# Softmax attention with a highway layer on one core: batch 1's attention moved behind the first chunk's products, its query scaled by head halves on two engines, and the last output tiles on more banks

## The chip, the cores and the metric

The kernel runs on one core of one Trainium2 chip. The metric is device time in microseconds. A core has TensorE (PE, which multiplies and transposes into PSUM), VectorE (DVE), ScalarE (ACT), GpSimd (POOL) and SyncE (SP, which here issues nearly all transfers); each works through its own list of instructions in order, and waits on semaphores where a result of another engine is needed.

## The reference

q, k and v have 8 batches, 8 heads, 576 positions and 64 features. The result of the attention goes, position by position, through a highway layer of width 512 (8 heads by 64).

```python
q_s = softmax(q, axis=-1)            # over the 64 features
k_s = softmax(k, axis=2)             # over the 576 positions
kv  = einsum('bhsd,bhse->bhde', k_s, v)
x   = einsum('bhsd,bhde->bhse', q_s, kv)   # then to [8*576, 512]
H   = maximum(x @ w_h, 0)
T   = sigmoid(x @ w_t + b_t)
out = T * H + (1 - T) * x
```

## The kernel before

A batch's q, k and v come as one tile each: 64 position groups of two heads on the 128 partitions, and 4 head pairs by 9 positions by 64 features in a row. Matmuls take 16-bit inputs.

Attention of batch `b`, by helper:

- `exp_half(b, which, a)`: ACT takes the exponential of one half of q or k (`eq`, `ek`), two head pairs at a time.
- `q_sums(b, a)`: DVE sums the 64 features of one half (tile `r32`). `q_scale_v` (batches 0 to 2) takes the reciprocal, copies it to 16 bits (`r2`) and scales all of `eq` on DVE in two pieces, 1024 and 1280 elements; from batch 3 on, POOL scales (`q_recip`, `q_scale_p`).
- `cast_v`: POOL converts v in halves to `v16`.
- `q_trans(b, g)`: PE transposes `eq` in three groups of positions (4, 4 and 1; tiles `pq`), and DVE copies each into `qsT`.
- `kv_half`, `kv_norm`: PE multiplies k and v (`psk`), DVE normalises it into `kvn`.
- `x_pair`, `x_left`: PE multiplies `qsT` and `kvn` (`px`). For the first 8 position groups the result goes to `xT`, three casts by ACT and one by DVE; the ninth group of every batch is collected in `x9`.

The highway layer works on nine chunks: chunk `c` below 8 is batch `c`'s `xT`, chunk 8 is `x9`. For each of four output blocks `ob`, `gate` has PE multiply by the gate's weights (`pt`) and ACT take a tanh in place, `carry` has PE multiply by the other weights (`ph`) and DVE form `dd = max(ph, 0) - x`, and `blend` has DVE form `g = (th + 1) * dd`. `out_tile(g, n)` turns x and half of `g` of two batches back into rows on PE (tile `nat`, eight matmuls in a pair of weights each), ACT copies it to `o32`, and after four tiles SP sends 1 MB off. `turn9` and `finish9` do that for chunk 8, with one `o9` tile for each pair of batches and transfers issued by SP and ACT.

PSUM has eight banks: four of `ps_ht` (tag `ht`) for `pt` and `ph`, three of `ps_q` (tag `qx`) for `pq`, `psk` and `px`, and one of `ps_nat` (tag `nat`). Tiles of a tag take its banks in turn, and a bank is free again once its last reader is done.

The order is written out by hand. `at(p, ...)` puts work at a place in a list, with place `8*c + 2*ob` for the gate of chunk `c` and block `ob`, the next for its carry, and two later its blend; the attention of batch `b` lies between the products of chunk `b - 1`. The list is then run once, which sets the order on every engine. Tiles of loaded data have three buffers for each of q, k and v; SP's loads run ahead as far as those allow.

Of the kernel before, what the change touches and what calls it, by code (L numbers as in the profile page):

```python
# [9 lines left out]
FP32 = mybir.dt.float32  # L10
FP16 = mybir.dt.float16
# [7 lines left out]
def kernel(  # L19
# [19 lines left out]
    def heads_view(t, b):  # L39
# [3 lines left out]
    consts = pool("consts", 1)  # L43
# [3 lines left out]
    small = pool("small", 2)  # L47
# [4 lines left out]
    og = pool("og", 2)  # L52
    ps_ht = pool("ps_ht", 4, space=PSUM)
    ps_q = pool("ps_q", 3, space=PSUM)
    ps_nat = pool("ps_nat", 1, space=PSUM)
# [4 lines left out]
        o, l, r, start=st, stop=sp, skip_group_check=True  # L60
    )

    def ptrans(o, i):
        nc.tensor.matmul(  # L64
            o, i, ident, is_transpose=True, start=True, stop=True,
            skip_group_check=True,
        )
# [9 lines left out]
    x9 = consts.tile([P, 4, B, 64], FP16, name="x9")  # L77
    g9 = consts.tile([P, 4, B, 64], FP16, name="g9")
# [68 lines left out]
    ek, eq, psk, qsT = {}, {}, {}, {}  # L147
# [45 lines left out]
    qsum = {}  # L193
# [9 lines left out]
    def q_scale_v(b):  # L203
# [7 lines left out]
        for s in (slice(0, 16), slice(16, 4 * N9)):  # L211
            nc.vector.tensor_mul(e[:, s], e[:, s], rb[:, s])  # L212

    def q_recip(b):
        nc.vector.reciprocal(qsum[b], qsum[b])  # L215

# [3 lines left out]
        r = qsum[b][:, s]  # L220
        nc.gpsimd.tensor_mul(e, e, r.broadcast_to(list(e.shape)))  # L221
# [90 lines left out]
    o32 = {}  # L312
    rows = out.rearrange("(g p n) m -> g p n m", g=B // 2, n=N9)

    def turn_block(t, k_, xs, us):
        dst = t[:, k_, :]
        mm(dst, xs, ident, True, False)
        mm(dst, us, half_i, False, True)

    def flat(t):  # L320
        return t.rearrange("p k d -> p (k d)")

    def out_tile(g, n):
# [9 lines left out]
        nc.scalar.copy(o32[g, n // 4][:, n % 4, :], flat(t))  # L333
# [4 lines left out]
    nat9 = {}  # L338

    def turn9(k_):  # L340
        for g in range(B // 2):
            if k_ == 0:
                ps, tag = (ps_q, "qx") if g < 3 else (ps_ht, "ht")
                nat9[g] = ps.tile([P, 4, P], FP32, tag=tag, name=f"nat9_{g}")
            blk = lambda t: t[:, k_, 2 * g : 2 * g + 2].rearrange("p b d -> p (b d)")
            turn_block(nat9[g], k_, blk(x9), blk(g9))

    o9 = {}

    def finish9(ks):  # L350
        c = slice(128 * ks[0], 128 * ks[-1] + 128)
        for g in range(B // 2):
            if g not in o9:
                o9[g] = og.tile([P, 512], FP32, tag="o9", bufs=4, name=f"o9_{g}")
            if g % 2:
                nc.vector.tensor_copy(o9[g][:, c], flat(nat9[g])[:, c])
            else:
                nc.scalar.copy(o9[g][:, c], flat(nat9[g])[:, c])
            (nc.sync, nc.scalar)[g % 2].dma_start(rows[g][:, NM, c], o9[g][:, c])


    events = {}
# [23 lines left out]
    for k_ in range(4):  # L386
        at(8 * B + 2 * k_ + 2, E(turn9, k_))
    at(8 * B + 7, E(finish9, (0, 1, 2)))
    at(8 * B + 8, E(finish9, (3,)))

    for b in range(1, B):
        p = 8 * (b - 1)
        s = p + {1: -1, 2: -2, 3: -4}.get(b, -5)
        if b > 1:
            at(s, E(exp_half, b, "q", 0))
        at(s + 1, E(exp_half, b, "q", 1), E(q_sums, b, 0))
        at(s + 2, E(q_sums, b, 1))
        if b <= 2:
# [25 lines left out]
    for f in [  # L424
        E(warm_up, 20),
        E(exp_half, 0, "q", 0), E(q_sums, 0, 0),
        E(exp_half, 0, "q", 1), E(q_sums, 0, 1),
        E(q_scale_v, 0),
        E(exp_half, 0, "k", 0), E(cast_v, 0, 0),
        E(exp_half, 0, "k", 1), E(cast_v, 0, 1),  # L430
        E(q_trans, 0, 0), E(q_trans, 0, 1), E(warm_up, 2), E(q_trans, 0, 2),
        E(warm_up, 6),
        E(kv_half, 0, 0), E(gate_bias), E(warm_up, 2), E(kv_half, 0, 1), E(kv_norm, 0),
        E(warm_up, 4),
        E(x_pair, 0, 0), E(warm_up, 2), E(x_pair, 0, 1), E(warm_up, 2), E(x_left, 0),
        E(warm_up, 2),
        *[E(cast_weight, "t", k_, nc.vector) for k_ in range(4)],
        *[E(cast_weight, "h", k_, (nc.gpsimd, nc.vector)[k_ // 3]) for k_ in range(4)],
        E(exp_half, 1, "q", 0),
    ]:  # L440
        f()
# [34 lines left out]
```

## Time and profile before

| | |
|---|---|
| median of 7 runs | 150.5 us (150.26 to 150.72) |
| the profiled execution | 150.53 us, of which the span is 148.6 us |
| busy in the span | PE 122.9 us (83%), DVE 107.0 (72%), ACT 89.5 (60%), POOL 40.6 (27%) |
| granted clock of PE, mean | 0.964 |
| transfers | 40.06 MB, of which 30.41 MB read and 9.44 MB written |

The span runs from the first to the last instruction. A busy share is an average over the whole of it, and the stages differ: the first third loads and starts up, the middle runs one chunk after another, and the last 20 us finish the last pair of batches and chunk 8.

### The profile page before, as it was taken

Reading aid. Unit: us, or ns where it says so; the run is one execution under the profiler, and the core shown is the slowest. Engines: PE = TensorE matmul, PEld = TensorE weight load, DVE = VectorE, ACT = ScalarE, POOL = GpSimd, SP = SyncE. Lnnn points to the kernel's source line nnn. Section 1 sums busy time; section 2 is a strip of 40 time slices with the busy share of each in tenths; the row PEclk is TensorE's granted clock in tenths of the full one; section 3 lists DMA queues with packets and bytes.
Section 4 is the critical chain, followed back from the end, with each engine's and each line's share of the span. In section 5 each row is a group of like instructions: output and inputs, shape, how many; then the busy total and the mean of one; then the engine's idle time right before and its main releaser. Section 6 shows DMA issues by size and latency. Waiting matters only on the chain.

```text
span 148.6 us, 3513 instructions
## 1 busy us (share of the span) xinstructions
PE 122.9 (83%) x1465; PEld 65.7 (44%) x1465; DVE 107.0 (72%) x199; ACT 89.5 (60%) x129; POOL 40.6 (27%) x36
## 2 busy tenths in 40 slices
PE   4949973496888987979998998999899999876830
PEld 2335221253335344536644654664474555454410
DVE  1593568977899997997799889889986766412361
ACT  3660417075771977698697787969737554546420
POOL 2006140302300039349207904920960000000000
PEclk9999999869789999999999999999999999999995
DMA  5999999999999999202999999920150060525544
GB/s 167 369 400 375 387 406 414 410 413 414 402 413 409 404 409 414 97 0 110 277 412 406 302 374 403 402 82 0 55 234 4 0 282 0 238 99 232 236 172 157
DMA packets 16118, 40.06 MB, mean 270 GB/s; under 512 B 740, under 2 KB 1768, under 8 KB 15080
## 3 DMA queue, kind: packets, MB, share of 16 engines
q1 hardware_dynamic: 15528, 39.33, 69.1%
q10 hardware_dynamic: 576, 0.52, 1.1%
q8 instruction: 11, 0.18, 0.4%
q14 instruction: 3, 0.02, 0.0%
HBM read 30.41 MB, written 9.44 MB: 268 GB/s over the span
## 4 chain that ended last, share of the span: by engine, by line
PE 48%; DVE 26%; DMA 11%; ACT 5%; issue 3%; SPq 3%; POOL 2%; ACTq 0%; POOLq 0%; DVEq 0%
PE pt L59 15%; PE ph L59 14%; DMA q<-in_q_dram 11%; DVE r L199 10%; PE nat L59 9%; PE pq L64 4%; DVE dd L299 4%; PE psk L59 4%; DVE g L307 3%; DVE xT L259 2%; SPq L92 2%; ACT o L333 2%; POOL eq L221 2%; PE px L59 1%; DVE eq L212 1%
## 5 line engine op out<-in xcount | busy, mean ns | idle before, releaser
L290 ACT ACTIVATE pt<-pt,bt 128x512 f32<-128x512 f32 x36 | 23.9, 662 | 30.9 <-PE pt L59 30.9
L59 PE MATMUL pt<-xT,w16t 128*128 128x512 f16 x128 | 35.8, 397 | 2.7 <-DVE xT L259 1.3
L59 PE MATMUL ph<-xT,w16h 128*128 128x512 f16 x128 | 34.4, 393 | 0.0
L221 POOL TENSOR_TENSOR eq<-eq,r 128x1024 f16<-128x1024 f16 (+1 forms) x10 | 20.9, 2115 | 40.0 <-DVE r L215 40.0
L299 DVE SCALAR_TENSOR_TENSOR dd<-ph,xT 128x512 f16<-128x512 f32 x32 | 21.9, 685 | 6.9 <-PE ph L59 6.6
L199 DVE TENSOR_REDUCE r<-eq 128x18 f32<-128x1152 f16 x16 | 21.5, 1344 | 5.7 <-ACT eq L154 5.6
L307 DVE SCALAR_TENSOR_TENSOR g<-pt,dd 128x512 f16<-128x512 f32 x36 | 24.4, 679 | 1.5
L161 POOL CAST v<-v 128x1152 f16<-128x1152 f32 x15 | 16.8, 1146 | 24.7 <-DMA v<-in_v_dram 24.7
L154 ACT ACTIVATE eq<-q 128x1152 f16<-128x1152 f32 x16 | 18.7, 1166 | 6.9 <-DMA q<-in_q_dram 6.9
L59 PE MATMUL nat<-half_i,g 128*128 128x128 f16 x144 | 19.9, 220 | 2.9 <-DVE g L307 2.9
L333 ACT COPY o<-nat 128x512 f32<-128x512 f32 x32 | 18.9, 591 | 4.7 <-PE nat L59 4.0
L59 PE MATMUL nat<-ident,xT 128*128 128x128 f16 x128 | 17.7, 219 | 3.1 <-ACT o L333 3.1
L59 PEld LDWEIGHTS <-w16t 128*128 128x128 f16 x144 | 12.7, 100 | 16.7 <-issue 3.2
L154 ACT ACTIVATE ek<-k 128x1152 f16<-128x1152 f32 x16 | 18.4, 1167 | 1.8 <-DMA k<-in_k_dram 1.8
L64 PE MATMUL pq<-ident,eq 128*128 128x128 f16 x144 | 12.5, 225 | 7.9 <-DVE eq L212 7.0
L59 PEld LDWEIGHTS <-g 128*128 128x128 f16 x144 | 14.0, 98 | 10.6 <-issue 3.8
L257 ACT CAST xT<-px 128x512 f16<-128x512 f32 x24 | 13.4, 593 | 7.5 <-PE px L59 7.3
L59 PEld LDWEIGHTS <-w16h 128*128 128x128 f16 x144 | 12.6, 101 | 12.0 <-issue 3.0
L235 DVE COPY qsT<-pq 128x1024 f16<-128x1024 f16 (+1 forms) x24 | 13.2, 553 | 4.1 <-PE pq L64 3.9
L64 PEld LDWEIGHTS <-eq 128*128 128x128 f16 x144 | 9.6, 100 | 12.6 <-issue 5.5
L59 PEld LDWEIGHTS <-xT 128*128 128x128 f16 x128 | 12.5, 97 | 5.1 <-issue 2.1
L59 PE MATMUL warm<-wide,ident 128*128 128x512 f16 x40 | 11.3, 421 | 1.9 <-DVE wide L140 1.9
(39 smaller groups left out, 82.9 us busy)
## 6 DMA issues: line engine op xcount, KB each, us to landing
out_dram<-o SPq DMA_DIRECT2D x8, 1024.0 KB, 4.7
q<-in_q_dram SPq DMA_DIRECT2D x7, 1152.0 KB, 14.4
k<-in_k_dram SPq DMA_DIRECT2D x7, 1152.0 KB, 14.6
v<-in_v_dram SPq DMA_DIRECT2D x6, 1152.0 KB, 14.6
v<-in_v_dram SPq DMA_DIRECT2D x4, 576.0 KB, 11.0
q<-in_q_dram SPq DMA_DIRECT2D x2, 576.0 KB, 4.0
k<-in_k_dram SPq DMA_DIRECT2D x2, 576.0 KB, 7.0
w32t<-in_moe_w_t_dram SPq DMA_DIRECT2D x1, 1024.0 KB, 10.8
```

What stands on the lines that cost most here:

```text
L59: mm = lambda o, l, r, st, sp: nc.tensor.matmul(o, l, r, start=st, stop=sp, skip_group_check=True)
L64: nc.tensor.matmul(o, i, ident, is_transpose=True, start=True, stop=True, skip_group_check=True,)
L154: nc.scalar.activation(dst[b][:, :, 2 * a : 2 * a + 2, :], in32[which][b][:, 2 * a : 2 * a + 2].rearrange("p c n d -> p n c d"), AF.Exp,)
L161: (eng or nc.gpsimd).tensor_copy(v16s[b % 2][:, :, 2 * a : 2 * a + 2, 0:64], in32["v"][b][:, 2 * a : 2 * a + 2].rearrange("p c n d -> p n ...
L199: nc.vector.reduce_sum(qsum[b][:, :, h], eq[b][:, :, h, :], axis=AX.X)
L221: nc.gpsimd.tensor_mul(e, e, r.broadcast_to(list(e.shape)))
L235: nc.vector.tensor_copy(qsT[b][:, :, n0:n1, :], t[:, :, 0:w, :])
L257: nc.scalar.copy(dst, t[c])
L290: nc.scalar.activation(ps, ps, AF.Tanh, bias=bt2[:, ob : ob + 1], scale=0.5)
L299: nc.vector.scalar_tensor_tensor(dd, ps, 0.0, xv(ob), op0=ALU.max, op1=ALU.subtract)
L307: nc.vector.scalar_tensor_tensor(gv(ob), th, 1.0, dd, op0=ALU.add, op1=ALU.mult)
L333: nc.scalar.copy(o32[g, n // 4][:, n % 4, :], flat(t))
```

## The change

Batch 1. Its query is summed, inverted and scaled by halves of heads: POOL scales the first half (`q_scale_half` with `nc.gpsimd`), DVE the second, in two instructions of 576 elements. All of chunk 0's products come ahead of its transposes, its k and v products and `px`. The middle group of its transposes is copied by ACT, and both halves of its v are converted by POOL (before, DVE converted one). Its k exponentials come one place later.

Batch 2. Both halves of its query's exponential, which lay a place or two earlier, now come behind chunk 1's first gate, its k exponentials two places later, and its transposes and products one place later.

The end. Tiles `nat` of the last pair of batches use the three `qx` banks beside `nat` (`spare`), and DVE copies every second one. Chunk 8's turns all come behind its products: `most9` turns three of four blocks into four banks, `last9` the fourth block of all pairs into one bank. All goes to one tile `o9`, and SP sends it in two transfers.

```diff
+    def q_scale_half(b, a, eng):
+        h = slice(2 * a, 2 * a + 2)
+        r32 = qsum[b][:, :, h]
+        nc.vector.reciprocal(r32, r32)
+        if eng is nc.gpsimd:
+            e = eq[b][:, :, h, :]
+            eng.tensor_mul(e, e, r32.broadcast_to(list(e.shape)))
+            return
+        r2 = small.tile([P, N9, 2, 2], FP16, tag="r2h", bufs=1, name=f"r2_{b}_{a}")
+        nc.vector.tensor_copy(r2, r32.broadcast_to([P, N9, 2, 2]))
+        e = eq[b][:, :, h, :].rearrange("p n c (w t) -> p n c w t", t=2)
+        for c in range(2):
+            rb = r2[:, :, c].unsqueeze(2).broadcast_to([P, N9, 32, 2])
+            nc.vector.tensor_mul(e[:, :, c], e[:, :, c], rb)
...
-    def q_trans(b, g):
+    def q_trans(b, g, eng=None):
...
-        nc.vector.tensor_copy(qsT[b][:, :, n0:n1, :], t[:, :, 0:w, :])
+        if eng is nc.scalar:
+            nc.scalar.copy(qsT[b][:, :, n0:n1, :], t[:, :, 0:w, :])
+        else:
+            nc.vector.tensor_copy(qsT[b][:, :, n0:n1, :], t[:, :, 0:w, :])
...
-    def out_tile(g, n):
+    def out_tile(g, n, spare=False):
...
-        t = ps_nat.tile([P, 4, P], FP32, tag="nat", name=f"nat_{g}_{n}")
+        ps, tag = (ps_q, "qx") if spare and n % 4 < 3 else (ps_nat, "nat")
+        t = ps.tile([P, 4, P], FP32, tag=tag, name=f"nat_{g}_{n}")
...
-        nc.scalar.copy(o32[g, n // 4][:, n % 4, :], flat(t))
+        o = o32[g, n // 4][:, n % 4, :]
+        if spare and n % 2:
+            nc.vector.tensor_copy(o, flat(t))
+        else:
+            nc.scalar.copy(o, flat(t))
...
+    def most9():
         for g in range(B // 2):
...
+            ps, tag = (ps_q, "qx") if g < 3 else (ps_nat, "nat")
+            t = ps.tile([P, 4, P], FP32, tag=tag, name=f"nat9_{g}")
+            for k_ in range(3):
+                turn_block(t, k_, blk9(x9, g, k_), blk9(g9, g, k_))
+            o = o9[:, g, 0:384]
+            if g % 2:
+                nc.vector.tensor_copy(o, flat(t)[:, 0:384])
+            else:
+                nc.scalar.copy(o, flat(t)[:, 0:384])
+        nc.sync.dma_start(rows9[:, :, 0:384], o9[:, :, 0:384])
+
+    def last9():
+        t = ps_ht.tile([P, 4, P], FP32, tag="ht", name="nat9_l")
         for g in range(B // 2):
...
+            turn_block(t, g, blk9(x9, g, 3), blk9(g9, g, 3))
+        nc.scalar.copy(o9[:, 0:2, 384:512], t[:, 0:2])
+        nc.vector.tensor_copy(o9[:, 2:4, 384:512], t[:, 2:4])
+        nc.sync.dma_start(rows9[:, :, 384:512], o9[:, :, 384:512])
...
-                at(p + 1 + i // 2, E(out_tile, g, i))
...
+                at(p + 1 + i // 2, E(out_tile, g, i, True))
+    at(8 * B + 8, E(most9), E(last9))
...
+    at(7, E(q_trans, 1, 0), E(q_trans, 1, 1, nc.scalar), E(q_trans, 1, 2))
...
+            2: ((3, 4, 5), (4, 5), (6, 7, 7)),
```

DVE, from the first sum of batch 1's query (`r32_1`, `eq_1`) on, before:

```order
L199 TENSOR_REDUCE r32_1_351<-eq_1_341 128x9x2
L299 SCALAR_TENSOR_TENSOR dd_0_0_370<-ph_0_0_365,xT_0_298 128x512
L199 TENSOR_REDUCE r32_1_351<-eq_1_341 128x9x2
L206 RECIPROCAL r32_1_351<-r32_1_351 128x36
L208 CAST r2_1_373<-r32_1_351 128x72
L212 TENSOR_TENSOR eq_1_341<-eq_1_341,r2_1_373 128x1024
L212 TENSOR_TENSOR eq_1_341<-eq_1_341,r2_1_373 128x1280
L307 SCALAR_TENSOR_TENSOR g_0_343<-pt_0_0_344,dd_0_0_370 128x8x64
L299 SCALAR_TENSOR_TENSOR dd_0_1_390<-ph_0_1_385,xT_0_298 128x512
L235 COPY qsT_1_392<-pq_1_0_393 128x4x256
L307 SCALAR_TENSOR_TENSOR g_0_343<-pt_0_1_378,dd_0_1_390 128x8x64
```

and now:

```order
L317 SCALAR_TENSOR_TENSOR dd_0_0_369<-ph_0_0_364,xT_0_299 128x512
L199 TENSOR_REDUCE r32_1_371<-eq_1_342 128x9x2
L217 RECIPROCAL r32_1_371<-r32_1_371 128x9x2
L325 SCALAR_TENSOR_TENSOR g_0_344<-pt_0_0_345,dd_0_0_369 128x8x64
L317 SCALAR_TENSOR_TENSOR dd_0_1_387<-ph_0_1_382,xT_0_299 128x512
L199 TENSOR_REDUCE r32_1_371<-eq_1_342 128x9x2
L217 RECIPROCAL r32_1_371<-r32_1_371 128x9x2
L223 CAST r2_1_1_391<-r32_1_371 128x36
L227 TENSOR_TENSOR eq_1_342<-eq_1_342,r2_1_1_391 128x9x64 x2
L325 SCALAR_TENSOR_TENSOR g_0_344<-pt_0_1_375,dd_0_1_387 128x8x64
L317 SCALAR_TENSOR_TENSOR dd_0_2_407<-ph_0_2_402,xT_0_299 128x512
```

Chunk 0's first blend is ahead of the scaling now, the second still behind it, and the copies of the transposes (`qsT_1`) have moved further down.

ACT, from the tanh of chunk 0's third block to that of chunk 1's second, before:

```order
L290 ACTIVATE pt_0_2_403<-pt_0_2_403,bt2_102 128x512
L154 ACTIVATE ek_1_410<-k32_1_125 128x9x128 x2
L290 ACTIVATE pt_0_3_435<-pt_0_3_435,bt2_102 128x512
L154 ACTIVATE eq_2_481<-q32_2_353 128x9x128
L257 CAST xT_0_298<-px_1_0_0_531 128x8x64
L257 CAST xT_0_298<-px_1_0_1_532 128x8x64
L257 CAST xT_0_298<-px_1_1_0_539 128x8x64
L154 ACTIVATE eq_2_481<-q32_2_353 128x9x128
L290 ACTIVATE pt_1_0_562<-pt_1_0_562,bt2_102 128x512
L154 ACTIVATE ek_2_575<-k32_2_355 128x9x128 x2
L290 ACTIVATE pt_1_1_593<-pt_1_1_593,bt2_102 128x512
```

and now:

```order
L308 ACTIVATE pt_0_2_395<-pt_0_2_395,bt2_102 128x512
L154 ACTIVATE ek_1_409<-k32_1_125 128x9x128
L308 ACTIVATE pt_0_3_412<-pt_0_3_412,bt2_102 128x512
L154 ACTIVATE ek_1_409<-k32_1_125 128x9x128
L251 COPY qsT_1_428<-pq_1_1_439 128x4x256
L275 CAST xT_0_299<-px_1_0_0_532 128x8x64
L275 CAST xT_0_299<-px_1_0_1_533 128x8x64
L275 CAST xT_0_299<-px_1_1_0_540 128x8x64
L308 ACTIVATE pt_1_0_560<-pt_1_0_560,bt2_102 128x512
L154 ACTIVATE eq_2_567<-q32_2_352 128x9x128 x2
L308 ACTIVATE pt_1_1_585<-pt_1_1_585,bt2_102 128x512
```

Batch 2's query (`eq_2`) has moved behind the tanh of chunk 1's first gate, and one half of batch 1's k (`ek_1`) behind that of chunk 0's last gate.

DVE, from chunk 8's first `dd` to the end, before:

```order
L299 SCALAR_TENSOR_TENSOR dd_8_0_2121<-ph_8_0_2116,x9_107 128x512
L307 SCALAR_TENSOR_TENSOR g9_108<-pt_8_0_2098,dd_8_0_2121 128x512
...
L299 SCALAR_TENSOR_TENSOR dd_8_3_2275<-ph_8_3_2270,x9_107 128x512
L356 COPY o9_1_2280<-nat9_1_2175 128x384
L356 COPY o9_3_2286<-nat9_3_2181 128x384
L307 SCALAR_TENSOR_TENSOR g9_108<-pt_8_3_2255,dd_8_3_2275 128x512
L356 COPY o9_1_2280<-nat9_1_2175 128x128
L356 COPY o9_3_2286<-nat9_3_2181 128x128
```

and now:

```order
L325 SCALAR_TENSOR_TENSOR g9_108<-pt_8_0_2101,dd_8_0_2124 128x512
L354 COPY o32_3_0_2126<-nat_3_3_2164 128x512
L317 SCALAR_TENSOR_TENSOR dd_8_1_2180<-ph_8_1_2175,x9_107 128x512
L354 COPY o32_3_4_2182<-nat_3_5_2193 128x512
...
L317 SCALAR_TENSOR_TENSOR dd_8_3_2250<-ph_8_3_2245,x9_107 128x512
L325 SCALAR_TENSOR_TENSOR g9_108<-pt_8_3_2238,dd_8_3_2250 128x512
L376 COPY o9_141<-nat9_1_2261 128x384
L376 COPY o9_141<-nat9_3_2277 128x384
L386 COPY o9_141<-nat9_l_2286 128x2x128
```

The large copies of `o9` have moved behind the last blend, and copies of `o32` have come in between `dd` and `g9`.

More of the change, by code (lines that the diff above doesn't have):

```diff
@@ L336, in out_tile, with blk9 @@
             nc.sync.dma_start(rows[g][:, 4 * i : 4 * i + 4, :], o32[g, i])
-    nat9 = {}
-    def turn9(k_):
-        for g in range(B // 2):
[L342 to L351, printed above, removed]
-        for g in range(B // 2):
[L353 to L359, printed above, removed]
+    o9 = consts.tile([P, 4, 512], FP32, name="o9")
+    rows9 = out.rearrange("(g p n) m -> n p g m", g=B // 2, n=N9)[NM]
+    def blk9(t, g, k_):
+        return t[:, k_, 2 * g : 2 * g + 2].rearrange("p b d -> p (b d)")
+    def most9():
+        for g in range(B // 2):
+            ps, tag = (ps_q, "qx") if g < 3 else (ps_nat, "nat")
[10 more added lines that the diff above has]
+        t = ps_ht.tile([P, 4, P], FP32, tag="ht", name="nat9_l")
+        for g in range(B // 2):
+            turn_block(t, g, blk9(x9, g, 3), blk9(g9, g, 3))
+        nc.scalar.copy(o9[:, 0:2, 384:512], t[:, 0:2])
+        nc.vector.tensor_copy(o9[:, 2:4, 384:512], t[:, 2:4])
+        nc.sync.dma_start(rows9[:, :, 384:512], o9[:, :, 384:512])
     events = {}
@@ L384 @@
             for i in range(8):
-                at(p + 1 + i // 2, E(out_tile, g, i))
[L386 to L391, printed above, removed]
+                at(p + 1 + i // 2, E(out_tile, g, i, True))
+    at(8 * B + 8, E(most9), E(last9))
+    at(0, E(exp_half, 1, "q", 1))
+    at(1, E(q_sums, 1, 0), E(q_scale_half, 1, 0, nc.gpsimd))
+    at(3, E(q_sums, 1, 1), E(q_scale_half, 1, 1, nc.vector))
+    at(5, E(exp_half, 1, "k", 0), E(cast_v, 1, 0))
+    at(6, E(exp_half, 1, "k", 1), E(cast_v, 1, 1))
+    at(7, E(q_trans, 1, 0), E(q_trans, 1, 1, nc.scalar), E(q_trans, 1, 2))
+    at(7, E(kv_half, 1, 0), E(kv_half, 1, 1), E(kv_norm, 1))
+    at(7, E(x_pair, 1, 0), E(x_pair, 1, 1), E(x_left, 1))
+    for b in range(2, B):
         p = 8 * (b - 1)
-        s = p + {1: -1, 2: -2, 3: -4}.get(b, -5)
-        if b > 1:
-            at(s, E(exp_half, b, "q", 0))
+        s = p + {2: 0, 3: -4}.get(b, -5)
+        at(s, E(exp_half, b, "q", 0))
         at(s + 1, E(exp_half, b, "q", 1), E(q_sums, b, 0))
         at(s + 2, E(q_sums, b, 1))
-        if b <= 2:
+        if b == 2:
             at(s + 2, E(q_scale_v, b))
```

9 lines of the change are left out of this document (2 added, 7 removed).

## The prediction

> **What bounds the kernel now.** I read the windows by stage first, then the waits, then the chain that ended last. In the fence below the columns are window and length, busy time of PE (with its instructions), granted clock, share of the DMA engines and GB/s; the last row, of another answer, has PE, PEld, DVE, ACT and POOL one after the other.
>
> ```profile
> span 148.6 us, 3513 instructions
> ...
> 21.80:25.20 3.40, 1.79 (x9) 1.00 1.04 411
> 25.20:28.60 3.40, 0.48 (x9) 1.00 1.04 411
> 28.60:32.00 3.40, 3.40 (x18) 0.50 1.04 411
> ...
> 35.40:38.80 3.40, 1.61 (x17) 1.00 1.04 405
> 38.80:42.30 3.50, 3.50 (x10) 0.51 1.04 412
> ...
> 60.00:127.00 67.00, 64.94 (x879) 36.81 (x876) 55.48 (x105) 49.87 (x76) 26.11 (x17) 1.00 0.51 188
> ```
>
> From 60 to 127 us PE is busy 64.94 of 67.0: it is the bound, the change moves nothing there, and whatever is won or lost ahead of it reaches the end whole. The two ends are different. Before 60 PE starves, and twice its clock is halved for about 3.4 us, each time right after a stretch with PE busy 1.61 us or less; after 1.79 us it was not halved. Who PE waits for (us in total, times, longest), early and late:
>
> ```profile
> PE pq L64 <- DVE eq L212: 5.0, 2, 4.5
> ...
> PE nat L59 <- ACT o L333: 3.1, 4, 0.8
> PE nat L59 <- DVE g L307: 2.9, 2, 2.3
> ```
>
> The first is batch 1's query, scaled by DVE ahead of chunk 0's remaining products. The other two lie behind 127 us: the output turns wait for the one `nat` bank that ACT empties, and the last blends of chunk 8 wait on DVE. The chain at the end (start, length):
>
> ```profile
> 125.97 0.45 PE nat L59 x8
> 126.42 0.78 PE ph L59 x4
> ...
> 138.17 0.88 PE ph L59 x4
> 139.05 0.02 issue
> 139.07 0.70 DVE dd L299
> ...
> 139.87 0.70 DVE g L307
> ...
> 140.62 0.56 PE nat L59 x7
> ...
> 143.70 0.61 DVE g L307
> ...
> 145.44 0.27 ACT o L358
> ```
>
> From the end of `ph_8_0` (127.2) to the last copy (145.71) are 18.5 us, and most steps that are not PE are waits which a second bank would remove.
>
> **The end, part by part.** The `nat` tiles of the last pair rotate over three `qx` banks and `nat`; by rotation each bank's copy is due about 2.6 us after its turn (two products and two turns), against a copy of some 0.6. Four of eight copies go to DVE, in the gaps between `dd` and `g`. So PE runs through. A turn is 0.45 us and a product about 0.87 (0.78 to 0.88 in the chain). From 127.2: 8 turns (3.6) and five products (4.35) bring `ph_8_3` to its start at 135.15. From a product's start to `dd` is 0.90 in the chain plus 0.15 that a chain piece starts late, so `dd_8_3` is at 136.2; `g` 0.80 later (139.07 to 139.87), at 137.0; the turn of `last9` 0.75 after that (139.87 to 140.62), at 137.75. The 24 matmuls of `most9` (1.35 by the turn's pace) fill PE's wait. Eight matmuls end at 138.35.
>
> Then DVE has two 384-wide copies after `g`, and the 256-wide one:
>
> ```profile
> L356 DVE COPY o<-nat 128x384 f32<-128x384 f32 x2 | 1.0, 546 | 0.0
> L358 ACT COPY o<-nat 128x384 f32<-128x384 f32 x2 | 1.0, 479 | 2.6 <-DVE o L356 2.3 <-PE nat L59 0.3
> ```
>
> `o9` of g=1 and 3: 137.6 to 138.65. The two last 256-wide copies read one bank and DVE's waits for ACT's in the built program: 0.4 each (below the 384-wide ones), 138.4 to 139.2. SP issues the large transfer at 138.65 and the small at 139.2, against 145.7 for the last issue before. But the last transfers are larger: 786 KB and 262 KB, where before half had left earlier. Below: size and us to landing; two windows of DMA (share of the engines, GB/s); SP's issues of them, first and last start.
>
> ```profile
> out_dram<-o SPq DMA_DIRECT2D x2, 192.0 KB, 2.0
> ...
> out_dram<-o SPq DMA_DIRECT2D x2, 64.0 KB, 1.6
> ...
> 142.00:143.00 1.00, 1.00 0.54 197
> ...
> 144.00:147.00 3.00, 0.61 0.87 284
> ...
> L359 SPq DMA_DIRECT2D out_dram<-o  x4: 332/332/333, 141.4 to 145.7; - x4
> ```
>
> Rows of 384 move at 197/0.54 = 364 KB per us of full share. The 852 KB of 144 to 147 took 2.61 us of it; three such transfers (590 KB) are 1.62, so the 262 KB in rows of 128 took 0.99. A landing is 2.0 - 0.54 = 1.46 fixed, plus 786/364 = 2.16: 142.3, and 143.3 with the small one behind it. Before: 145.7 + 1.6 = 147.3. The end gains **4.0 us**. Bounds: 4.9 if transfer and fixed part overlap as for a full 1 MB (no more than 0.9 of the 3.6), 3.0 if the second waits out its own fixed part in line (1.0 more). I keep the sum, which is in the middle. The two DMA issues leave ACT's queue; ACT has nothing behind them, so that is worth nothing by itself.
>
> **The start, part by part.** PE's list has the last two pairs of chunk 0's products ahead of batch 1's transposes. These rows are the yardsticks: DVE, POOL and ACT durations (mean ns of one after the bar), then single instructions in time.
>
> ```profile
> L221 POOL TENSOR_TENSOR eq<-eq,r 128x1024 f16<-128x1024 f16 (+1 forms) x10 | 20.9, 2115 | 40.0 <-DVE r L215 40.0
> ...
> L161 POOL CAST v<-v 128x1152 f16<-128x1152 f32 x15 | 16.8, 1146 | 24.7 <-DMA v<-in_v_dram 24.7
> ...
> L212 DVE TENSOR_TENSOR eq<-eq,r 128x1280 f16<-128x1280 f16 x3 | 2.5, 819 | 0.0
> ...
> L212 DVE TENSOR_TENSOR eq<-eq,r 128x1024 f16<-128x1024 f16 x3 | 2.1, 693 | 0.1
> ...
> L199 DVE TENSOR_REDUCE r<-eq 128x18 f32<-128x1152 f16 x16 | 21.5, 1344 | 5.7 <-ACT eq L154 5.6
> ...
> L154 ACT ACTIVATE eq<-q 128x1152 f16<-128x1152 f32 x16 | 18.7, 1166 | 6.9 <-DMA q<-in_q_dram 6.9
> ...
> L290 ACT ACTIVATE pt<-pt,bt 128x512 f32<-128x512 f32 x36 | 23.9, 662 | 30.9 <-PE pt L59 30.9
> ```
>
> ```profile
> 22.94 1.35 DVE L199 TENSOR_REDUCE r<-eq 128x18 f32<-128x1152 f16 x1 [2.05 <-ACT eq L154]
> ...
> 26.60 0.65 DVE L208 CAST r<-r 128x72 f16<-128x72 f32 x1
> 27.28 1.43 DVE L212 TENSOR_TENSOR eq<-eq,r 128x1024 f16<-128x1024 f16 x2
> ...
> 36.11 0.62 PE L59 MATMUL px<-qsT,kvn 64*64 64x512 f16 x5 [0.75 <-DVE kvn L188]
> ...
> 42.60 0.20 DVE L208 CAST r<-r 128x72 f16<-128x72 f32 x1
> 42.83 1.43 DVE L212 TENSOR_TENSOR eq<-eq,r 128x1024 f16<-128x1024 f16 x2
> ...
> 58.98 1.03 PE L59 MATMUL pt<-xT,w16t 128*128 128x512 f16 x4
> ```
>
> Up to `px_1`: DVE's first sum still starts at 22.94; then a short reciprocal, `g_0_0`, `dd_0_1`, the second sum (about 25.8 to 27.1), reciprocal, cast and two scalings of 576 elements (0.47 each, extrapolated from 693 and 819 ns). POOL scales the other half from 24.6 (2.1 us) and then casts both halves of v (1.15 each) until 29.1, beside DVE's work. The cast took 0.65 beside a POOL cast and 0.20 alone, so I add 0.5: `g_0_1` at 29.1. It frees the bank of `pt_0_3`, and from there one thing waits for the next: blend 0.7, product 1.0, tanh 0.65, `ek_1` 1.15 (ACT is in order, so its second half is behind that tanh), the new ACT copy of `qsT_1` about 1.05 (1166 ns for 1152 elements), two rounds of `psk` 0.9, reciprocals and `kvn` 0.8. That is 6.3: `px_1` at 35.4 against 36.11, **0.7 earlier**. The idle of 4.5 us was mostly cover for this same chain.
>
> From `px_1` to batch 2's scaled query: `eq_2` is now behind `pt_1_0`'s tanh on ACT, where before one half was done ahead. px and casts 2.5, product and tanh 1.7, first exponential 1.15, then on DVE sum 1.3, blend 0.6, sum 1.3, reciprocal and cast 0.6, two scalings 1.45: 10.6, so 46.0 against 44.26, **1.75 later**. PE meanwhile has one product more behind it, and then nothing.
>
> From there to `pt_2_2`: DVE does `dd_1_1`, three `qsT` copies and two blends, `kvn` of batch 2, the sums of batch 3, `dd_1_3` and only then the cast that chunk 2's first product needs, 9.1 us by the rows' pace; then three products, a turn, two groups of transposes to `pt_2_2`, 4.2. That is 13.3, so 59.3 against 58.98; before, 14.7 passed, with a stall for POOL's scaling. Net: **0.3 later** at the place from which PE is the bound. Ends: 0.7 earlier if the scalings are untouched by POOL and the reciprocals run at once, 1.3 later if both scalings wait out a whole cast.
>
> `v`'s casts go behind the scaling on POOL and end at 29.1, 4 us ahead of `psk`: hidden. `eq_2` frees its input buffer some 3 us later than before; the DMA share is 1.04 in every early window, so loads queue on the engines rather than on SP's waits, and I cost that at nothing; uncovered, it would first show in chunk 5's load.
>
> A third term is the clock. PE is idle for about 3.7 us between `ph_1_1` and batch 2's transposes (41.7 to 45.4). The rows show that 1.61 us busy in 3.4 was followed by half speed, so a half-speed stretch there, over `pt_1_2`, `psk` and `ph_1_2`, is likely. Its price lies between 0 (the stretch of 38.8 to 42.3 was followed by PE still waiting for DVE) and 1.35 (the whole delay of `ph_1_2`, for which `dd_1_2` waits). I take 0.5, since in this stretch too DVE mostly ends the waits.
>
> The Trainium skill, "TensorE: Matmul & The Clock Gate", section "What's actually happening", says that the clock drops to half after at least one idle window of about 3.4 us. By that the 1.61 us window would have kept the clock; the trace differs. By the page this term would be 0, by the rows up to 1.35.
>
> **Sum.** 148.6 - 4.0 + 0.3 + 0.5 = 145.4 of span; the profiled execution took 150.53 for 148.6, 1.93 around it: **147.3 us**. The median shown, 150.5, is the same within 0.03. Under 0.2% (0.3 us) I call no change.
>
> **Rivals.**
> 1. The clock costs more: full 1.35, and a second stretch while PE waits 2 us for `xT_1` ahead of `pt_2_0` (up to 1.7). For it: the two halvings of before. Against: products stand in that window. 147.3 - 0.5 + 1.35 to 3.05 = 148.2 to 149.9.
> 2. DVE's scaling is shut out by POOL: both wait for the casts to 29.15, 1.0 later, and all behind it: 148.3. For it: 0.65 against 0.20. Against: the casts come one by one. The Trainium skill, "SBUF — State Buffer", section "Who interferes with whom", states it as a rule: an instruction of DVE with two SBUF inputs and one of GpSimd that reads SBUF exclude each other for the whole instruction.
> 3. The start gains: scaling at 28.5, no half speed on the path, turning +0.8 into -0.7: 145.8. For it: 0.8 us of v's cast and a copy leave DVE. Against: `eq_2` comes later.
> 4. Slower: half speed persists from 45.7 over three stretches to 56, 1.7 each, since PE does little in every one: 5.1 against the 0.5 taken gives 151.9. It decides from 3.7 us lost to half speed in all, more than two full stretches.
>
> **Chances.** Forecast 0.52, with its own range 146.4 to 148.1; rival 1 0.20, 2 0.10, 3 0.14, 4 0.04. From 145.7 to 149.2 leaves out about half of rival 3, the upper part of rival 1 and rival 4, under 2 in 10. Faster 0.94, same 0.02, slower 0.04.
>
> **What would show it.** PE's `nat` waits for ACT should go from 3.1 to near 0 and `ph_8_3` to the last copy should take about 4 us; the last two transfers should end some 4 us after the first is issued. `px_1` near 35.4, batch 2's scaling ending near 46, a half-clock row around 45.7 to 49.1, `pt_2_2` near 59.5 to 60. I am wrong if `pt_2_2` lies outside 58.3 to 61, or if the large transfer holds the end beyond 146 us.

## The result, and the profile after

The changed kernel takes 149.29 us (median of 12 runs, 146.04 to 152.44), the kernel before 150.59 (31 runs, 149.75 to 151.54). The ratio is 0.9714 with a 95% interval of 0.9668 to 0.9759; like the ratios of the experiments it is formed over the runs within 1.5% of the kernel's fastest, here 146.04 and 146.70, and by the medians it is 149.29/150.59 = 0.991. So it is faster, as forecast. By the ratio the time is 146.3 us, 1.0 below the forecast of 147.3; the median lies 2.0 above it and 0.1 above the top of the range.

The profiled execution took 149.73 us, 147.6 of it span (mean clock 0.959), against 150.53 and 148.6. Of the kernel after, PE's busy time by window (window and length, PE busy and instructions, granted clock, DMA share, GB/s):

```profile
26.18:29.59 3.41, 0.83 (x4) 1.00 1.04 413
29.59:33.00 3.41, 2.82 (x15) 0.50 1.04 413
39.83:43.24 3.41, 1.67 (x8) 1.00 1.04 411
43.24:46.66 3.42, 1.22 (x12) 1.00 1.04 407
46.66:50.07 3.41, 3.41 (x50) 0.50 1.04 411
53.48:56.90 3.42, 1.66 (x17) 1.00 1.04 412
56.90:60.31 3.41, 3.41 (x12) 0.50 0.94 372
63.40:130.40 67.00, 64.95 (x878) 1.00 0.50 186
```

The last row is the bound of before, unchanged: 64.95 us busy in 67, against 64.94. But three stretches run at half speed ahead of it, where before had two: after windows with 0.83, 1.22 and 1.66 us busy, but not after one with 1.67. Whom PE waits for, in total, times and longest:

```profile
PE pq L64 <- DVE eq L212: 5.5, 2, 3.9
PE ph L59 <- DVE g L325: 3.6, 2, 3.2
PE pt L59 <- DVE xT L277: 2.6, 4, 1.3
...
PE nat L59 <- DVE g L325: 0.5, 1, 0.5
```

PE's 3.1 us of waits for ACT's `nat` copies are gone, and those for `g` at the end fell from 2.9 to 0.5. Steps of the start, then of the end, from the timeline (start, length, idle time before it in brackets):

```profile
26.75 2.46 POOL L161 CAST v<-v 128x1152 f16<-128x1152 f32 x2
27.49 2.04 DVE L227 TENSOR_TENSOR eq<-eq,r 128x576 f16<-128x576 f16 x2
...
35.35 0.61 PE L59 MATMUL px<-qsT,kvn 64*64 64x512 f16 x5 [0.61 <-DVE kvn L188]
...
44.61 1.43 DVE L212 TENSOR_TENSOR eq<-eq,r 128x1024 f16<-128x1024 f16 x2
...
62.35 1.03 PE L59 MATMUL pt<-xT,w16t 128*128 128x512 f16 x4
...
136.74 0.58 ACT L356 COPY o<-nat 128x512 f32<-128x512 f32 x1 [3.13 <-DMA out_dram<-o]
...
136.86 0.69 DVE L354 COPY o<-nat 128x512 f32<-128x512 f32 x1 [1.97 <-PE nat L59]
...
142.52 0.38 SPq L379 DMA_DIRECT2D out_dram<-o  x1
143.04 0.41 SPq L387 DMA_DIRECT2D out_dram<-o  x1
```

Two rows are new beside the plan: DVE's two scalings take 2.04 us beside POOL's casts of v, and ACT waits 3.13 us for the landing of an output transfer before it may write the `o32` buffer again. DVE's copy of `nat_3_5` at 136.86 writes the same buffer. The row puts its wait of 1.97 us down to PE, but that turn had ended by 135.1, and the trace has DVE and ACT wait for the same landing until 136.7. The output transfers' size and time to landing, and the end of the chain that ended last:

```profile
out_dram<-o SPq DMA_DIRECT2D x8, 1024.0 KB, 5.1
...
out_dram<-o SPq DMA_DIRECT2D x1, 768.0 KB, 3.4
out_dram<-o SPq DMA_DIRECT2D x1, 256.0 KB, 3.6
```

```profile
136.92 0.55 issue
137.47 0.68 DVE g L325
138.15 0.60 DVE o L354
138.74 0.61 DVE dd L317
139.44 0.69 DVE g L325
140.14 0.61 DVE dd L317
140.84 0.70 DVE g L325
141.59 0.58 PE nat_l L59 x7
142.19 0.38 ACT o L385
142.59 0.42 DVE o L386
```

The chain at the end runs over DVE from 136.92 on: the blends of chunk 8 stand behind the late copy of `nat_3_5` in DVE's list. From `ph_8_3` (138.37) to the end of the last copy it is 4.6 us, forecast was about 4.

The place from which PE is the bound, `pt_2_2`, splits the span. In the kernel before it starts at 58.98 of 148.6, so 89.6 us follow; in the changed kernel at 62.35 of 147.6, so 85.2 follow. **The end gained 4.4 us and the start lost 3.4**; together 1.0, the difference of the spans. All experiments are read at this place (times in us from one execution each; "half" is the number of 3.41 us stretches at half speed ahead of it; "issue" is SP's first of the two last transfers):

| kernel | half | pt_2_2 | issue | span | pt_2_2 to issue | pt_2_2 to end |
|---|---|---|---|---|---|---|
| before | 2 | 58.98 | - | 148.6 | - | 89.6 |
| after | 3 | 62.35 | 142.52 | 147.6 | 80.17 | 85.2 |
| e1 old start, new end | 2 | 59.56 | 139.95 | 145.3 | 80.39 | 85.7 |
| e2 new start, old end | 4 | 62.70 | - | 152.0 | - | 89.3 |
| e3 third output buffer | 2 | 60.13 | 139.71 | 144.7 | 79.58 | 84.6 |
| e4 gaps filled | 0 | 58.45 | 138.03 | 143.1 | 79.58 | 84.6 |
| e5 e1, PE's list 80 rows longer | 2 | 60.08 | 139.65 | 146.1 | 79.57 | 86.0 |
| e6 e4 with more, shorter fills | 0 | 58.41 | 138.59 | 143.6 | 80.18 | 85.2 |
| e7 old start filled, new end | 0 | 57.77 | 137.34 | 142.7 | 79.57 | 84.9 |
| e8 e4, all scaling on POOL | 0 | 57.36 | 136.93 | 142.0 | 79.57 | 84.6 |
| e9 e1 with one bank | 2 | 58.95 | 142.42 | 147.8 | 83.47 | 88.9 |
| e10 only later gaps filled | 3 | 62.10 | 141.67 | 146.7 | 79.57 | 84.6 |
| e11 e8 and third buffer | 0 | 57.77 | 137.34 | 142.4 | 79.57 | 84.6 |
| e12 e4 again | 0 | 59.22 | 138.80 | 143.8 | 79.58 | 84.6 |

### The profile page after: what moved, and what is told of

Its sections match the earlier page's. It is cut to its first block, busy times and chain, and to the rows that moved or that the text cites. A ratio compares the mean times of both kernels' runs of the same rounds, so it can differ in the third digit from the quotient of the medians.

```text
span 147.6 us, 3509 instructions
## 1 busy us (share of the span) xinstructions
PE 123.4 (84%) x1465; PEld 67.2 (46%) x1465; DVE 108.6 (74%) x201; ACT 88.0 (60%) x125; POOL 43.9 (30%) x38
## 4 chain that ended last, share of the span: by engine, by line
PE 56%; DVE 31%; ACT 4%; DMA 3%; issue 2%; SPq 0%; DVEq 0%; ACTq 0%
PE pt L59 16%; PE ph L59 16%; DVE r L199 11%; PE nat L59 9%; PE pq L64 6%; PE psk L59 5%; DVE g L325 4%; DVE dd L317 4%; DMA q<-in_q_dram 3%; PE warm L59 3%; PE px L59 2%; DVE xT L277 2%; ACT eq L154 2%; DVE w16t L111 2%; DVE kvn L188 1%
## 5 line engine op out<-in xcount | busy, mean ns | idle before, releaser
L59 PE MATMUL pt<-xT,w16t 128*128 128x512 f16 x128 | 35.2, 390 | 3.9 <-DVE xT L277 2.6
L59 PE MATMUL ph<-xT,w16h 128*128 128x512 f16 x128 | 35.3, 402 | 3.6 <-DVE g L325 3.6
L161 POOL CAST v<-v 128x1152 f16<-128x1152 f32 x16 | 18.2, 1160 | 17.1 <-DMA v<-in_v_dram 10.2
L59 PE MATMUL nat<-half_i,g 128*128 128x128 f16 x140 | 19.0, 220 | 0.5 <-DVE g L325 0.5
L356 ACT COPY o<-nat 128x512 f32<-128x512 f32 x28 | 16.5, 591 | 3.8 <-DMA out_dram<-o 3.1
L275 ACT CAST xT<-px 128x512 f16<-128x512 f32 x24 | 13.3, 592 | 7.7 <-PE px L59 7.5
L253 DVE COPY qsT<-pq 128x1024 f16<-128x1024 f16 (+1 forms) x23 | 12.5, 548 | 4.5 <-PE pq L64 4.3
L64 PEld LDWEIGHTS <-eq 128*128 128x128 f16 x144 | 10.3, 105 | 9.5 <-ACT ek L154 6.4
L59 PE MATMUL warm<-wide,ident 128*128 128x512 f16 x40 | 11.8, 436 | 1.9 <-DVE wide L140 1.9
```

What stands on the lines that cost most here:

```text
L59: mm = lambda o, l, r, st, sp: nc.tensor.matmul(o, l, r, start=st, stop=sp, skip_group_check=True)
L64: nc.tensor.matmul(o, i, ident, is_transpose=True, start=True, stop=True, skip_group_check=True,)
L161: (eng or nc.gpsimd).tensor_copy(v16s[b % 2][:, :, 2 * a : 2 * a + 2, 0:64], in32["v"][b][:, 2 * a : 2 * a + 2].rearrange("p c n d -> p n ...
L275: nc.scalar.copy(dst, t[c])
L356: nc.scalar.copy(o, flat(t))
```

## The experiments

The kernel before ran beside each set: 150.53 us (e1 to e4), 151.18 (e5 to e8), 150.77 (e9 to e12). Ratios are to these.

**One part alone: e1 and e2.** e1 has the order of the start as before and the new end; e2 the reverse.

```diff
e1, against after:
-    at(0, E(exp_half, 1, "q", 1))
-    at(1, E(q_sums, 1, 0), E(q_scale_half, 1, 0, nc.gpsimd))
...
-    for b in range(2, B):
+    for b in range(1, B):
...
e2, against after:
-                at(p + 1 + i // 2, E(out_tile, g, i, True))
-    at(8 * B + 8, E(most9), E(last9))
+                at(p + 1 + i // 2, E(out_tile, g, i))
+    for k_ in range(4):
+        at(8 * B + 2 * k_ + 2, E(turn9, k_))
+    at(8 * B + 7, E(finish9, (0, 1, 2)))
+    at(8 * B + 8, E(finish9, (3,)))
```

> The new end with the start as before (batch 1 and 2 as in the kernel before). Theory A (the start of the change gives nothing and brings half-speed stretches that differ from run to run): 146.0 to 147.5 us, with little scatter, the clock near 0.964 as before, so faster than the whole change's median of 149.3. Theory B (the start of the change is worth something and the scatter comes from the end): above 148 us, with scatter as wide as that of the whole change.

> The new start with the end as before. Theory A: 150.5 to 154 us, scattered by some 5 us from run to run in step with the granted clock. Theory B: 148.5 to 150.5 us, with no more scatter than before (about 1 us).

e1: 147.22 us (146.61 to 147.38), ratio 0.9753 [0.9715, 0.9792]. e2: 153.79 us (152.43 to 155.84), ratio 1.0168 [1.0108, 1.0227]. By the medians the end alone gains 3.3 us and the start alone loses 3.3 (3.7 and 2.5 by the ratios). The change is two changes of opposite sign.

**The output buffer: e3.** The last 1 MB goes through a buffer of its own, a free input buffer of v.

```diff
-            o32[g, n // 4] = og.tile([P, 4, 512], FP32, tag="o32", name=f"o32_{g}_{n}")
+            if g == 3 and n == 4:
+                spare_v = ld.tile([P, 4, N9, 64], FP32, tag="v32", name="o32_last")
...
+            else:
+                o32[g, n // 4] = og.tile([P, 4, 512], FP32, tag="o32", name=f"o32_{g}_{n}")
```

> The whole change, with the last group of four output tiles in a third buffer (an input buffer that is free by then), so that its first copy on ACT no longer waits for the landing of the transfer two groups earlier. Theory A (that wait, 3.13 us in the profile of the changed kernel, holds PE and DVE up in chunk 8): about 2 to 3 us below the whole change at the same clock, 146 to 147 us at a clock of 0.96. Theory C (the end is bound by PE and the last transfers, the wait is hidden): the same as the whole change, within 0.5 us at the same clock.

148.53 us (146.72 to 150.59), ratio 0.9782 [0.973, 0.9833]; the scatter is as wide as that of the changed kernel. ACT's wait for the transfer is gone, and from `pt_2_2` to the issue it is 79.58 us against 80.17. So the wait of 3.1 us was worth 0.6, nearer to theory C than to theory A.

**The clock: e4, and e12 again.** 44 matmuls of 512 columns, whose result nobody reads, stand in PE's three gaps of the start.

```diff
+    def fill(n):
+        t = ps_nat.tile([P, 512], FP32, tag="nat", name="fill_t")
+        for _ in range(n):
+            mm(t, ident, wide, True, True)
...
+    at(6, E(fill, 12))
-    at(7, E(q_trans, 1, 0), E(q_trans, 1, 1, nc.scalar), E(q_trans, 1, 2))
+    at(7, E(q_trans, 1, 0), E(q_trans, 1, 1, nc.scalar), E(q_trans, 1, 2), E(fill, 3))
...
+    at(11, E(fill, 16))
...
+    at(15, E(fill, 8))
```

> The whole change with 44 idle-time matmuls (results never read) in PE's gaps of the start, so that the clock is not halved; nothing else is moved. Theory A (each half-speed stretch costs 1 to 1.5 us): clock at 0.98 or above, 145 to 146.5 us, scatter under 1 us. Theory D (PE is not what limits the start, DVE is, and the clock only goes along): the clock rises, and the time stays within 0.5 us of the median of the whole change, 149.3 us.

> The changed kernel with all three early gaps filled, once more, on the same chip as the two runs ahead of it. Expected 144.8 to 145.4, as in its first run (144.96). It gives the distance to the version with POOL's scaling and the third buffer: 0.7 to 1.5 us if DVE's scalings beside POOL's casts were on the path (theory D), within 0.4 if not.

e4: 144.96 us (144.61 to 145.12), ratio 0.9608 [0.9571, 0.9644]; e12: 145.02 us (144.76 to 145.96), ratio 0.9629 [0.9586, 0.9671]. Work that computes nothing took 4.3 us off the median of the changed kernel, and most of its scatter. Of e4, PE by window, then two rows of the timeline:

```profile
20.00:60.00 40.00, 37.23 (x376) 1.00 1.04 408
```

```profile
34.37 0.60 PE L59 MATMUL px<-qsT,kvn 64*64 64x512 f16 x4
...
58.45 1.03 PE L59 MATMUL pt<-xT,w16t 128*128 128x512 f16 x4
```

The granted clock is 1.00 throughout, and `pt_2_2` comes 3.9 us earlier than in the changed kernel; from `px_1` it takes 24.08 us, against 27.00. So half speed cost the changed kernel 3.9 us ahead of `pt_2_2`. It cost the old start something too: e7 below says how much.

**A transfer that lands late: e5 and e6.** The 1 MB transfer for which ACT waits landed after 6.1 us in the changed kernel (6.3 in e1), where in e4 none of the last ones took more than 3.9. The packets of the instruction queue tell why. These are packets of 16384 bytes, late in the program (start in us; time taken in ns; the output transfers in flight near it):

```
after  131.66  1644   inside the 1 MB issued at 130.6
e1     128.88  1876   inside the 1 MB issued at 127.8
e6     127.64  1739   inside the 1 MB issued at 126.6, landing after 6.1 us
e5     140.33  1164   inside the 768 KB issued at 139.65
e4     123.46, 137.29  between transfers
```

The page of the changed kernel has 11 of them over the program (packets, MB, share of the DMA engines):

```profile
q8 instruction: 11, 0.18, 0.5%
```

PE has 2,930 matmuls and weight loads there, one packet for some 270; that points to PE's list of instructions. e5 moves it by 80 rows of that list, e6 by some 256 against the changed kernel.

```diff
e5, against e1:
+    def tiny(n):
+        for _ in range(n):
+            mm(warm[:, 0:1], ident, wide[:, 0:1], True, True)
...
-        E(warm_up, 20),
+        E(warm_up, 20), E(tiny, 40),
e6, against e4 (128 fills in the place of 44):
-            mm(t, ident, wide, True, True)
+            mm(t[:, 0:176], ident, wide[:, 0:176], True, True)
...
-    at(6, E(fill, 12))
+    at(6, E(fill, 35))
```

> The new end with the old start, plus 40 one-column matmuls with their weight loads among the warm-up matmuls: PE's list is 80 rows longer, and the fetch of PE's next instructions, which took 1.9 us in the middle of the 1 MB transfer of the pair before last when only the end was changed, should fall elsewhere. Nothing else changes; the 40 matmuls stand where PE has no work yet. Theory F (the fetch delays that transfer, and the 3.3 us that ACT then waits for its buffer lie on the path): that transfer's landing falls from 6.3 to about 5 us, ACT's wait for it to under 1.5 us, and the time from 147.2 to 145.2 to 146.4. Theory G (the last products and blends set the end, ACT's wait lies beside them): the wait goes, and the time stays at 147.2 within 0.3. If the wait stays at 3 us, the fetch is not what causes it.

> The kernel with PE's early gaps filled, but with 128 matmuls of 176 columns in the place of 44 of 512: the same columns and the same places, and a PE list that is longer than that of the changed kernel by a number of rows close to one whole fetch, so that a fetch should fall in the last large transfers again. The clock should stay whole until 127 us as with the long fill. Theory F (fetch on the path): a transfer with a landing of 6 us and a wait of ACT of about 3 us come back, and the time goes from 145.0 to 146.5 to 148. Theory G (beside the path): they come back and the time stays within 0.4 of 145.0. If no fetch falls in a transfer, this run tells nothing on F and G, and only repeats the fill.

e5: 146.85 us (145.75 to 148.16), ratio 0.9689 [0.9631, 0.9746]. e6: 146.09 us (145.79 to 147.27), ratio 0.9677 [0.9623, 0.9731]. In e5 ACT's wait for a transfer is gone. In e6 it is back:

```profile
ACT o L356 <- DMA out_dram<-o: 3.1, 1, 3.1
```

The wait follows the packet's place, so the fetch of instructions makes it. Its price up to the issue is 0.6 to 0.8 us (80.18 and 80.39 against 79.58), not the 3 that ACT waits: theory F had the cause, theory G was nearer to the price, though that is not zero. By the ratios the price is 1.0 us both times (e1 against e5, e6 against e4), with intervals that overlap. In e5's profiled execution the packet fell into the last transfers instead, which nothing hides (size and us to landing, 3.4 and 3.6 elsewhere):

```profile
out_dram<-o SPq DMA_DIRECT2D x1, 768.0 KB, 4.6
out_dram<-o SPq DMA_DIRECT2D x1, 256.0 KB, 4.7
```

From `pt_2_2` to the end that run took 86.0 us against 84.6, 1.4 more.

**The old start with its gaps filled: e7.**

```diff
against e1, with fill as in e4:
+    at(3, E(fill, 18))
...
+        if b == 1:
+            at(p + x[0], E(fill, 2))
...
+        if b == 1:
+            at(p + x[1], E(fill, 2))
```

> The new end with the old start, and fill matmuls in the old start's gaps: 18 after the matmul product of batch 1's first query, 2 each after the first two products of keys for that batch. It asks what the new start is worth once the clock is held. Theory A (the new start gives nothing by itself, its half-speed stretches cost 3 us): with the clock held, both starts give the same, 144.6 to 145.4, against 145.0 for the new start with its gaps filled. Theory B (the new start is worth 0.7 us or more when PE is at full speed): 145.7 to 146.5 here. If only one of the old start's two half-speed stretches goes, 146 to 147 says nothing between them, and the clock rows are to be read first.

144.76 us (144.6 to 145.52), ratio 0.9584 [0.9542, 0.9627], against 0.9608 and 0.9629 for the new start filled. So the new start gains nothing with the clock held either (theory A). By the ratios it is worse by 0.0024 to 0.0045 of 150.6, that is 0.4 to 0.7 us, with intervals that overlap; the traces show 0.7. Counted from the start of DVE's first sum of batch 1's query, which differs between executions, `pt_2_2` comes after 34.88 us in e7 (22.89 to 57.77) and after 35.57, 35.59 and 35.58 in e4, e6 and e12. The same count is 36.04 in the kernel before and 39.47 in the changed kernel. So half speed cost 1.2 us with the old start and 3.9 with the new one, and of the 3.4 us that the start lost 2.7 are clock and 0.7 the new order itself.

**DVE's scaling beside POOL: e8, and e11 with the third buffer.**

```diff
e8, against e4 (e11 has e3's buffer too):
-    at(3, E(q_sums, 1, 1), E(q_scale_half, 1, 1, nc.vector))
+    at(3, E(q_sums, 1, 1), E(q_scale_half, 1, 1, nc.gpsimd))
```

> The new start with its gaps filled, and both halves of batch 1's query scaled on POOL, in the place of one on DVE. DVE's two scalings took 2.04 us beside POOL's casts, 1.1 more than their size makes them, and the second blend of chunk 0 stands behind them. Theory D (these scalings are on the path up to the place where PE is the bound): the blend starts about 2 us earlier, the first product of keys for batch 1 waits for POOL or comes up to 1.5 us earlier, and the time goes from 145.0 to 143.5 to 144.5. Rival: POOL's two halves end later than DVE's, v's casts come 2 us later and so does the product of keys, and the time stays at 145.0 within 0.3 or rises.

> The version to which the runs point: the new start with its gaps filled, both halves of batch 1's query scaled on POOL, and the last output tile of four in a buffer of its own, so that no copy waits for the landing of an earlier transfer. Expected: 143.6 to 144.2, 0 to 0.5 below the version without the third buffer (144.1), since no fetch of instructions fell in a transfer there. If the third buffer costs anything (its space is a free input buffer of v), 144.2 to 144.8.

e8: 144.13 us (144.04 to 145.48), ratio 0.9563 [0.9501, 0.9625]; e11: 144.26 us (143.98 to 144.46), ratio 0.9562 [0.9526, 0.9597]. Beside e12, on the same chip, e11 is 0.76 us faster (144.26 against 145.02). Of e8:

```profile
26.96 0.63 DVE L325 SCALAR_TENSOR_TENSOR g<-pt,dd 128x512 f16<-128x512 f32 x1
...
33.28 0.60 PE L59 MATMUL px<-qsT,kvn 64*64 64x512 f16 x4
```

The second blend starts at 26.96 instead of 29.45, and `px_1` 1.1 us earlier than in e4 (34.37), though POOL ends later. The same 1.1 stands at `pt_2_2` (57.36 against 58.45). Of it 0.2 is an earlier start of DVE's first sum (22.69 against 22.88); counted from there it is 0.9 at both places, and e11 against e12 gives 0.9 too (23.10 to 57.77, 23.64 to 59.22). DVE's scaling beside the casts was on the path. The times show 0.7 to 0.8 of it. The third buffer adds nothing here, since no transfer landed late. e8 and e11 are the best of all versions, 4.4% below before.

**Where the end's gain sits: e9.**

```diff
against e1:
-        ps, tag = (ps_q, "qx") if spare and n % 4 < 3 else (ps_nat, "nat")
-        t = ps.tile([P, 4, P], FP32, tag=tag, name=f"nat_{g}_{n}")
+        t = ps_nat.tile([P, 4, P], FP32, tag="nat", name=f"nat_{g}_{n}")
```

> The new end with the old start, but the eight nat tiles of the last pair have one bank again, with four of eight copies on DVE as in the changed kernel, and the last turns and transfers as changed. It tells what of the 3.3 us that the new end gained (150.5 to 147.2) is the banks. Theory H (the banks carry the gain: the 3.1 us that PE waited for ACT's copies were on the path): PE's waits for nat copies come back with 3 us or more, DVE's 692 ns copies making them a little longer than before, and the time is 149.6 to 150.6. Theory I (the last turns and the merged transfers carry it): 147.2 to 148.2.

149.91 us (149.32 to 151.06), ratio 0.9953 [0.9917, 0.9988]. PE's waits for the copies are back:

```profile
PE nat L59 <- ACT o L355: 2.9, 4, 0.7
```

From `pt_2_2` to the end it takes 88.9 us, against 84.6 with four banks and 89.6 before. Of the 5.0 us that the end gains where no copy waits for a landing, the banks carry 4.3, the last turns and merged transfers 0.7 (theory H).

**Which stretch costs: e10.** e4 without the fills at places 6 and 7.

```diff
against e4:
-    at(6, E(fill, 12))
...
-    at(7, E(x_pair, 1, 0), E(fill, 2), E(x_pair, 1, 1), E(fill, 1), E(x_left, 1))
+    at(7, E(x_pair, 1, 0), E(x_pair, 1, 1), E(x_left, 1))
```

> The changed kernel with fills only in the two later gaps (16 matmuls ahead of batch 2's transposes, 8 ahead of the first product of chunk 2); the gap before batch 1's transposes stays empty. It asks which of the half-speed stretches cost the time. Expected: the first stretch, near 29.6 to 33.0, comes back as before, those near 46.6 and 56.9 do not. Theory A1 (each stretch costs about the same, 1.3 us): 146.2 to 146.6. Theory A2 (the first lies under DVE's chain and costs little, the later ones carry the loss): 145.0 to 145.6. Theory A3 (the first delays batch 1, and everything behind it, by the 1 us that px_1 moved between the fill and the changed kernel): 145.7 to 146.2.

148.11 us (145.55 to 148.93), ratio 0.9734 [0.9665, 0.9803]. Neither of A1 to A3, since the stretches did not stay where the expectation had them:

```profile
26.91:30.32 3.41, 0.25 (x3) 1.00 1.04 411
30.32:33.74 3.42, 3.42 (x21) 0.50 1.05 415
33.74:37.15 3.41, 1.91 (x84) 1.00 1.04 411
37.15:40.56 3.41, 2.98 (x16) 0.50 1.04 405
40.56:43.98 3.42, 3.42 (x9) 0.50 1.04 411
```

Two more came behind the first, where none had been in the changed kernel, and `pt_2_2` is at 62.10. Its fastest run, 145.55, had a mean clock of 0.992, the slowest, 148.93, one of 0.949. The price of a single stretch by its place is left open.

## Why the prediction was right and wrong

**The end: right in size, with two errors that cancel.** The 4.0 us were worked out up to the last landing: 143.3, that is 84.3 us behind `pt_2_2`, and measured 143.04 + 3.6 - 62.35 = 84.3. By span it is 4.4, since 1.0 us instead of 1.3 follows the last landing. The issue of the large transfer was forecast 79.67 us behind `pt_2_2`: 79.57 or 79.58 in the eight kernels in which no copy waits for a landing. What was left out is the `o32` buffer: the step said "by rotation each bank's copy is due", and a copy also needs a free output buffer. That put 0.6 us on the issue (80.17). Mis-sized the other way were the last transfers: 3.6 us for the large and 4.1 for the small were forecast, 3.4 and 3.6 measured. Had no fetch fallen into the transfer, the end would have gained 5.0 us, just past the bound of 4.9.

**Up to `px_1`: right in sum only.** Forecast 35.4, measured 35.35. Inside, `g_0_1` came at 29.45 instead of 29.1, since the scalings took 2.04 us against 0.94, more than the 0.5 allowed for POOL. The 6.3 us from there were 4.9 in e4; in the changed kernel 5.9, because a half-speed stretch (29.59 to 33.00) covers the first product. It cost about 1.0 here (35.35 against 34.37), and was not in the sum. That the two errors cancel is luck.

The scalings bear out rival 2's mechanism. They lasted 0.72 and 1.39 us, and ended at 28.21 and 29.53; POOL's casts ended at 27.90 and 29.21. Each scaling ended some 0.3 us behind a cast. The Trainium skill, "SBUF — State Buffer", section "Who interferes with whom", has the two exclude each other; these rows agree. No run times these scalings without a cast beside them. The price of the rival, 1.0 later than forecast for all behind it, did not come: `g_0_1` was 0.35 late, as 0.5 for POOL stood in the sum already. e8's 0.9 is not that price either, since e8 takes the whole scaling off DVE.

**From `px_1` to batch 2's scaling: right.** 10.6 us were forecast, and 46.04 - 35.35 = 10.69 measured; the end at 46.0 was met.

**From there to `pt_2_2`: the work right, the clock wrong.** 13.3 us were forecast for the work; with the clock held it is 13.38 (45.07 to 58.45 in e4). In the changed kernel it is 16.31. The failed step is the third term, "I take 0.5": it measured 2.9, in two stretches, 46.66 to 50.07 where the text had put one, and 56.90 to 60.31, which the text had only in rival 1. That rival, held at 0.20, is what happened: it gave 148.2 to 149.9, and 149.73 in this execution and 149.29 as median came. Its counter-argument, that products stand in the window, failed: the window ahead of the stretch had PE busy for only 1.66 us. By the prediction's own sign, `pt_2_2` beyond 61, it was wrong at the start.

With the term at 2.9 the sum is 148.6 - 4.0 + 0.3 + 2.9 = 147.8 of span, 149.7 us, close to the profiled execution (147.6 and 149.73). The reason given for 0.5, that DVE mostly ends the waits there, does not hold: products, transposes and turns of PE lie between DVE's steps in that chain. DVE waits 1.69 us for `ph_1_2` there, against 0.35 in e4, and each stretch cost about 1.5 us.

**Costed at nothing.** The later exponential of batch 2, which frees an input buffer some 3 us later, did not show: 64.95 us busy in 67 from 63.4 on.

**The chances.** Rival 4's point of decision, 3.7 us lost to half speed, was reached (1.0 + 2.9 = 3.9 in this execution), but against an end that gained 4.4 it leaves 1.0. Runs with more half-speed time, down to a mean clock of 0.937, took 151.12 and 152.44, slower than before. The 0.94 for faster was given as if the changed kernel scattered as before does (1.8 us over 31 runs); it scatters over 6.4. At the other side two of the twelve runs, with the highest mean clocks (0.983 and 0.972), took 146.04 and 146.70, less than the forecast. So the term for the clock is not one number in this kernel: the 2.9 is that of the profiled execution.

## What to carry to other kernels

Where the bound engine starves at the start, read the granted clock beside its gaps, and price the stretches as part of the chain: a move that only lengthens a gap can cost more than the wait that it removes. Here 44 matmuls with no reader in such gaps took 4.3 us off the median. Where copies are given more PSUM banks, count the buffers they write to as well, and look for which transfer must land before each is free.

## What was not expected of the hardware

- **Half speed comes in whole stretches of 3.413 us, at a phase that differs between executions.** All lengths between clock changes in these traces, up to the last change, are multiples of it, and twelve runs of one kernel spread over 6.4 us, the slower the lower the clock: a straight line through them gives 1.3 us for 0.0116 of mean clock, one stretch. The Trainium skill, "TensorE: Matmul & The Clock Gate", section "What's actually happening", calls the window of 3413 ns free-running; the trace agrees.
- **PE's busy time in one window does not decide it.** The prediction read a limit between 1.61 and 1.79 us of 3.4 out of before's rows. In e3 two windows in a row with less kept full speed, and one with 2.13 lost it:

```profile
17.10:20.52 3.42, 2.13 (x15) 1.00 1.04 405
20.52:23.93 3.41, 3.41 (x9) 0.50 1.04 412
...
41.00:44.41 3.41, 1.50 (x7) 1.00 1.05 414
44.41:47.82 3.41, 1.37 (x14) 1.00 1.04 407
47.82:51.24 3.42, 3.42 (x93) 1.00 1.04 410
```

  What does decide it is open, but the records of the matmuls give a lead that no run tests. Estimate for each window the columns that PE's matmuls move through the array, a product on 64 by 64 of its 128 by 128 counted as a quarter. In e3 the window with 2.13 us has about 2,790 and the two kept ones 3,170 and 3,240; in the changed kernel 1.66 us, which lost full speed, is 2,550, and 1.67, which kept it, 3,580. Over all fourteen traces every full-speed window with 3,170 or more kept full speed, and those with 2,900 or less lost it, save two right behind a half-speed stretch (2,320 in e3 and 2,720 in the changed kernel). Half-speed windows of the start sort alike: half speed went on after 2,970 and less, and ended after 3,440 and more.
- **A fetch of instructions inside an output transfer makes that transfer land later.** A fetch of 16 KB inside an output transfer took 1.2 to 1.9 us (0.9 to 1.0 in most other places), and the transfer landed 1.2 to 2.4 us later (4.6 against 3.4, 6.3 against 3.9). Where a fetch falls moves with the number of PE's instructions (80 rows moved it out in e5, some 256 brought it back in e6), so any edit ahead of it can shift this cost in or out.
